# Two attention groups moved in a fused attention, mixture-of-experts and soft-routing kernel

## The chip, the cores and the metric

The kernel runs on one core of a Trainium2 chip, in one launch. The metric is device time in microseconds (us). Before the change the median of three runs is 650.23 us (649.72 to 650.28). The measurement of the changed kernel is set against it.

## What is computed

Three stages follow each other, all in fp32.

```
# attention: 4 batches, 8 heads, 768 positions, 64 per head; chunks of 32 queries
k_ctx = k[chunk start - 16 : chunk end + 8];  k_full = mem_k (8) + k_ctx
a = softmax(q_c @ k_full.T / 8);  out = a @ v_full
# squared-relu layer: x (3072, 512), w_in (512, 2048), w_out (2048, 512)
h = x @ w_in;  g = s * relu(h)**2 + b;  x = g @ w_out
# soft routing: 8 experts with 4 slots each
logits = x @ phi
slot_input = softmax(logits, over tokens).T @ x
slot_out[e] = relu(slot_input[e] @ w1[e]) @ w2[e]
out = softmax(logits, over slots) @ slot_out
```

For the two layers the kernel splits each operand into a high and a low part in the matmul format `float32r`, and a product is three matmuls: high by high, high by low, low by high.

## The kernel before, in words

**Tiling.** The 3072 tokens are six blocks j of 512. Attention is cut into units u: one block and one pair of heads, four units a block, 24 in all. The units of blocks 2 and 3 (8 to 15) are taken in the order of `SEQ`; unit 14 is block 3, head pair 1, unit 16 the first of block 4.

A unit has these parts. Its *scores* (`att_qk`) are 16 small fp32 matmuls, which the profile counts as 32, into one PSUM bank. Then comes the softmax on that bank: `att_top` on VectorE (two small masks where a batch ends, the maximum, the subtraction), the exponent on ScalarE (`att_e`), and `att_norm` on VectorE (sum, epsilon, reciprocal, multiplication). The *turn* (`att_turn`) is four transposes on TensorE, placed by two copies (`att_place`). The *values* (`att_pvmm`) are again 16 matmuls, counted as 32, and one ScalarE copy into x (`att_copy`). `run_bg("qk", u, bank)` issues the scores, the loads of Q and K two units on, and the whole softmax; `run_bg("pv", u, bank)` issues the values, the copy and the load of V two units on; "qktr" is the scores of u with the turn of u - 1 behind them.

**Steps.** Blocks 0 and 1 go through the squared-relu layer in 32 steps n, one for each block and each 128 columns of `w_in`. A step issues on TensorE `mm_h(n)` (12 matmuls of 512 columns into bank 4 or 5), then what attention is due, then `mm_y(n - 1)` (12 matmuls into banks 0 to 3). Between the two lie, for the h of the step, `make_r` (ScalarE), `make_t` (VectorE), `make_high` (ScalarE) and `make_low` (VectorE): the square, biased and split.

**Super blocks.** Blocks 2 and 3 are one 2 by 2 super block (`first_super`), blocks 4 and 5 another (`last_super`). A super block goes through eight pairs p of column blocks by a scheme of seven products of half size in place of eight: a11, s1, s2, s4, s3, a22, a12, six matmuls each (`prod`, with the operands from `x_split`, `x_sum`, `w_sums`, `w_split`). Products add onto each other in PSUM: bank A takes a11, is copied out (c11), takes s2 on top, is copied out (c12), takes s3 on top; bank C takes s1, is copied out (c22), takes s4 on top. The copies c11, c22 and c12 are ScalarE's (L808, L826, L833). The two products of the step before (`pending`) run between.

**Order.** TensorE and SP (the DMA queue's engine) run in written order everywhere. In steps 16 to 27 (`plain_step`) a planner orders the other engines. Steps 28 to 31 (`hand_step`) and the two super blocks stand under a manual schedule of ScalarE, VectorE and GpSimd too: they run in written order. What attention is due in which step is listed in `bg`. The lines around the change are:

```
# hand_step(31), L1343 on
mm_h; w_split(1, 0); make_r; values of unit 16; make_g; mm_y(30)
x_split t2; x_split t3; x_sum t4; w_split(2, 0)
# first_super, p = 0, L807 on
prod a11; c11; x_split t4; w_sums(1); w_split(3, 0); prod s1; c22; w_split(0, 1)
prod s2; c12; w_split(1, 1); scores of 17; prod s4; add; prod s3; add; softmax of 17
mm_y(31); prod a22; prod a12; turn of 17
```

In `hand_step`, values that lead a step's list are issued ahead of `make_g`. In step 28 they would write bank 5; in step 31 they write bank 7.

Of the kernel before, what the change touches and what calls it, by code (L numbers as in the profile page):

```python
# [18 lines left out]
NHP = 4  # L19
# [34 lines left out]
def tile_attention_moe_softmoe(  # L54
# [88 lines left out]
    bank = [ppool.tile([P, 512], F32, name=f"bank{i}", tag=f"bank{i}") for i in range(8)]  # L143
# [69 lines left out]
    def att_qk(u, b):  # L213
        S = b.rearrange("p (t n) -> p t n", t=8)
        qt, kt = qv(u), kv(u)
        for i in range(4):
            for z in range(2):
                for par in range(2):
                    c = 4 * i + 2 * par + z
                    pe.matmul(S[64 * par:64 * par + 64, 2 * i + z, :], lhsT=qt[:, c].rearrange("p h n -> p (h n)"), rhs=kt[:, KG * c:KG * c + 64],  # L220
                              start=True, stop=True)
# [19 lines left out]
    def att_exp(u, b):  # L241
        att_top(u, b)
        att_e(u)
# [11 lines left out]
    def att_norm(u, last=None):  # L255
        att_sum(u)
        att_mul(u, last or dve)
# [137 lines left out]
    def make_g(n):  # L395
        make_t(n)
        make_high(n)
        make_low(n)
# [173 lines left out]
    for u in range(2 * NHP, 4 * NHP + 1):  # L572
        n0 = NF - 4 + 2 * (u - 2 * NHP)
        bg[n0].append(("qk", u))
        bg[n0 + 2].append(("tr", u))
        bg[n0 + (4 if u < 4 * NHP - 2 else 3)].append(("pv", u))
    for step, task in ((3, "log"), (3, "ytr0"), (5, "etr"), (5, "ytr1"), (7, "ytr2"), (7, "ytr3"), (7, "csoft"), (9, "slot")):
        bg[NF + step].append((task, 0))
    for n, tasks in bg.items():
# [5 lines left out]
    def att_next(a):  # L585
        if a + 2 < NB * NHP:
            load_q(a + 2)
            load_k(a + 2)

    def run_bg(task, a, b=None):  # L590
        if task == "qk":
            att_qk(a, b)
            att_next(a)
            att_exp(a, b)
            att_norm(a)
        elif task == "tr":
            att_tr(a, b, a < 2 * NHP)
        elif task == "qktr":
            att_qk(a, b)
            att_next(a)  # L600
            c = mbank()
            att_turn(a - 1, c)
            att_place(a - 1, c)
            att_exp(a, b)
            att_norm(a)
        elif task == "pv":
            att_pv(a, b)
            att_low(a, b)
            if a + 2 < NB * NHP:
                load_v(a + 2)  # L610
        elif task == "log":
            y_logits(a, b)()
        elif task[:3] == "ytr":
            y_tr(int(task[3]), b, "act" if int(task[3]) % 2 else "dve")
        elif task == "etr":
            pe.transpose(b[:, 128:256], lts, ident)
            e_tr(b)
            dve.tensor_copy(lall[:, 4 * a:4 * a + 4, :], b[:, 128:256].rearrange("p (t s) -> p t s", t=4))
        elif task == "csoft":
            c_soft(a)  # L620
        elif task == "slot":
            slots(a, b)
# [138 lines left out]
    def first_super(pending):  # L761
# [41 lines left out]
        for p in range(NPR):  # L803
            c11 = hl(ch[0])[:, p % 2]
            more = p + 1 < NPR
            A, D = yq[0], yq[3]
            prod(A, "a11", "b11", p)  # L807
            act.activation(out=c11, in_=A, func=AF.Copy)  # L808
            if p == 0:
                x_split("t4", 0, 1)  # L810
            if p:
                att_place(4 * NHP + p, D)
                finish(p - 1)
            if p == 1:
                w_split(2, 1)
                evac_spare(yp)
            if p == 5:
                run_bg("csoft", jr)
            if more:
                w_sums(p + 1)  # L820
            w_split(3, p)
            wi_load(p + 2)
            if not more:
                t2_load(0)
            prod(C, "s1", "t1", p)
            act.activation(out=c22, in_=C, func=AF.Copy)  # L826
            w_prep(0, p + 1)
            if not more:
                prep(0)
                x_split("b11", 1, 0)  # L830
                x_split("b11", 1, 1)
            prod(A, "s2", "t2", p, False)
            act.activation(out=c12, in_=A, func=AF.Copy)  # L833
            w_prep(1, p + 1)
            if not more:
                t2_load(1)
            if p:
                run_bg("pv", 4 * NHP + p, B)
            if more:
                att_qk(4 * NHP + p + 1, D)  # L840
                att_next(4 * NHP + p + 1)
                if p:
                    att_exp(4 * NHP + p + 1, D)
                    att_norm(4 * NHP + p + 1)
            pending.pop(0)()
            if p:
                next_load(p, 0)
            prod(C, "s4", "b22", p, False)
            dve.tensor_tensor(out=c12, in0=C, in1=c12, op=ALU.add)
            if not more:  # L850
                x_sum("t1", 1, 0)
                x_sum("t1", 1, 1)
            prod(A, "s3", "t3", p, False)
            dve.tensor_tensor(out=c22, in0=A, in1=c22, op=ALU.add)  # L854
            if p == 0:
                att_exp(4 * NHP + 1, D)
                att_norm(4 * NHP + 1)

            def square2():
                relu(r2, ch[1])  # L860
                times(cur[G2[p]], ch[1], r2)
                if p:
                    w_prep(2, p + 1)

            if p:
                square2()
            if not more:
                t2_load(4)
                prep(1)
                x_split("t1", 1, 0)  # L870
                x_split("t1", 1, 1)
            late = lambda: None
            for t in routing.get(p, ()):
                if t == "log":
                    late = y_logits(jr, D)
                else:
                    run_bg(t, jr, B if t in ("ytr0", "ytr1", "ytr3") else D)
            pending.pop(0)()
            if p:
                next_load(p, 1)  # L880
            else:
                ws_load(R[3], 1)
            if not more:
                t2_load(6)
                t2_load(7)
            prod(A, "a22", "t4", p, False)
            relu(t21, A)
            times(t21, A, t21)
            late()
            prod(B, "a12", "b21", p)  # L890
            if not more:
                t2_load(5)
            dve.tensor_tensor(out=c11, in0=B, in1=c11, op=ALU.add)
            g_high(t21, G[1])
            relu(t11, c11)
            g_low(t21, G[1])
            times(t11, c11, t11)
            if p == 0:
                square2()
            if more:  # L900
                att_turn(4 * NHP + p + 1, D)
            pending.append(lambda p=p: mm_job(yp, cur[R[(2 * p) % 4]], G[1], p == 0, False))
            pending.append(lambda p=p: mm_job(yp, cur[R[(2 * p + 1) % 4]], G[0], False, p == NPR - 1))
# [327 lines left out]
    with tc.manual_schedule(engines={mybir.EngineType.PE, mybir.EngineType.SP}):  # L1231
# [101 lines left out]
        def hand_step(n):  # L1333
            m = n - (NSTEP - 4)
            if m == 0:
                split_wi(n + 1)
                wi_load(0)
                wi_load(1)
                ws_load(R[0], NPR, True)
                ws_load(R[1], 0, True)  # L1340
            split_wo(n)
            sp.dma_start(out=DWS[n % NF], in_=WO[n % 2])
            mm_h(n, (0, 1, 2, 3))  # L1343
            if m == 3:
                w_split(1, 0)
            make_r(n)
            tasks = [lambda t=t, a=a: run_bg(t, a, bank[7] if n == NSTEP - 1 else HB[(n + 1) % 2] if t == "pv" else mbank())
                     for t, a in bg[n]]
            if bg[n][0][0] == "pv":
                tasks.pop(0)()  # L1350
            make_g(n)
            if n + 2 < NSTEP:
                split_wi(n + 2)
            for t in tasks:
                t()
            mm_y(n - 1)
            if m == 0:
                x_sum("t1", 0, 1, pool)
            elif m == 1:
                x_split("t1", 0, 1)  # L1360
            elif m == 2:
                w_sums(0)
                x_sum("t2", 0, 1)
                x_sum("t3", 0, 1)
                x_split("b22", 0, 1)
                w_split(0, 0)
            else:
                x_split("t2", 0, 1)
                x_split("t3", 0, 1)
                x_sum("t4", 0, 1)  # L1370
                w_split(2, 0)
                ws_load(R[2], NPR + 1)
# [258 lines left out]
```

## Time and profile before

| | |
|---|---|
| median of three runs | 650.23 us |
| the profiled execution | 649.8 us, its span 648.0 us |
| TensorE matmul | busy 636.5 us, 98% |
| TensorE weight load | busy 511.6 us, 79%, beside the matmuls |
| VectorE | busy 441.0 us, 68% |
| ScalarE | busy 354.8 us, 55% |
| GpSimd | busy 281.2 us, 43% |
| DMA | 183.33 MB, mean 283 GB/s |
| granted TensorE clock | 0.997 of full speed |
| chain that ended last | TensorE 96%, VectorE 2% |

A matmul's row in the trace is longer than its share of the engine, since matmuls overlap: what one costs is the distance between two starts. In a timeline, rows of one line and one set of tiles that follow without a gap are one row with a count. A bracket at its end gives the engine's idle time before it and what released it. PE is TensorE, PEld its weight loads, DVE is VectorE, ACT ScalarE, POOL GpSimd.

### The profile page before, as it was taken

The page shows a single profiled execution, that of the slowest core. Times are in us where ns is not written, and L with a number is a line of the kernel's source. Part 1 is how long each engine was busy: PE and PEld are TensorE (multiplying, and loading weights), DVE is VectorE, ACT ScalarE, POOL GpSimd, SP SyncE. Part 2 cuts the span into 40 slices and gives each one's busy share as a digit, 9 for nine tenths or more (in the row PEclk, how much of TensorE's full clock was granted, in tenths as well). Part 3 has the DMA queues.
Part 4 walks back from the last instruction along what each step waited for, and adds up shares of the span by engine and source line. Part 5 has one row for each costly group of instructions (what it writes and reads, how often), then busy time and mean ns, then how long its engine had stood idle before and what let it go on. Part 6 is the DMA issues. An engine that isn't in the chain of part 4 may idle for free.

```text
span 648.0 us, 12886 instructions
## 1 busy us (share of the span) xinstructions
PE 636.5 (98%) x4965; PEld 511.6 (79%) x4965; DVE 441.0 (68%) x716; ACT 354.8 (55%) x640; POOL 281.2 (43%) x227
## 2 busy tenths in 40 slices
PE   8999999999999999999999999999999999999995
PEld 7788888888878888888788887888887888886384
DVE  6999989666864678656566587616766889676233
ACT  5898887655554556554354555425654456554232
POOL 5897856343333584643534103454455515320000
PEclk9999999999999999999999999999999999999998
DMA  8998854577746755978754687469999789999998
GB/s 331 408 405 306 307 184 171 170 274 252 262 168 212 286 200 211 332 263 297 285 192 180 218 294 227 183 196 379 333 344 323 243 291 334 331 379 409 406 408 323
DMA packets 59821, 183.33 MB, mean 283 GB/s; under 512 B 6640, under 2 KB 7920, under 8 KB 59760
## 3 DMA queue, kind: packets, MB, share of 16 engines
q1 hardware_dynamic: 59760, 182.51, 77.5%
q8 instruction: 39, 0.64, 0.4%
q14 instruction: 22, 0.18, 0.1%
HBM read 136.35 MB, written 46.14 MB: 282 GB/s over the span
## 4 chain that ended last, share of the span: by engine, by line
PE 96%; DVE 2%; ACT 0%; issue 0%; DVEq 0%; POOL 0%; POOLq 0%
PE bank L407 28%; PE bank L737 24%; PE bank L377 13%; PE bank L995 12%; PE bank L285 3%; PE bank L220 3%; PE bank L1486 2%; PE bank L1445 2%; PE bank L459 2%; PE bank L263 2%; PE bank L433 1%; PE bank L475 1%; PE bank L1515 1%; PE bank L1245 1%; PE bank L513 0%
## 5 line engine op out<-in xcount | busy, mean ns | idle before, releaser
L407 PE MATMUL bank<-g,wo 128*128 128x512 f32 x528 | 130.0, 395 | 0.0
L407 PEld LDWEIGHTS bank<-g,wo 128*128 128x128 f32 x528 | 96.9, 188 | 21.7 <-ACT wi L347 0.8
L377 PE MATMUL bank<-x,wi 128*128 128x512 f32 x384 | 92.8, 390 | 0.0
L377 PEld LDWEIGHTS bank<-x,wi 128*128 128x128 f32 x384 | 71.8, 188 | 15.3 <-DVE x L308 0.4
L385 DVE SCALAR_TENSOR_TENSOR rt<-bank,cons,rt 128x512 f32<-128x512 f32 x32 | 23.8, 745 | 29.1 <-ACT rt L381 28.9
L326 POOL TENSOR_SCALAR sp<-sp 128x512 f32<-128x512 f32 x20 | 43.0, 2174 | 0.0
L366 POOL TENSOR_TENSOR wo<-w,wo 128x512 fp32r<-128x512 f32 x16 | 21.9, 1367 | 45.3 <-ACT wo L362 32.5
L729 POOL TENSOR_TENSOR w14n<-sp6n,w14n 128x512 fp32r<-128x512 f32 x8 | 14.5, 1815 | 46.9 <-ACT w14n L728 46.9
L351 POOL TENSOR_TENSOR wi<-w,wi 128x512 fp32r<-128x512 f32 x17 | 22.4, 1318 | 24.8 <-ACT wi L347 21.3
L347 ACT ACTIVATE wi<-w 128x512 fp32r<-128x512 f32 x32 | 20.1, 629 | 19.9 <-PE bank L377 15.0
L392 DVE SCALAR_TENSOR_TENSOR g<-rt,cons,g 128x512 fp32r<-128x512 f32 x32 | 25.6, 799 | 6.2 <-ACT g L388 5.9
L362 ACT ACTIVATE wo<-w 128x512 fp32r<-128x512 f32 x32 | 20.1, 627 | 16.4 <-PE bank L407 9.0
L285 PEld LDWEIGHTS bank<-pb,v 128*64 128x64 f32 x704 | 22.2, 138 | 8.0 <-issue 2.5
L388 ACT ACTIVATE g<-rt,cons 128x512 fp32r<-128x512 f32 x32 | 23.1, 720 | 9.0 <-DVE rt L385 8.5
L239 ACT ACTIVATE ep<-ep 128x512 f32<-128x512 f32 x22 | 13.9, 632 | 23.1 <-DVE ep L235 23.0
L285 PE MATMUL bank<-pb,v 128*64 128x64 f32 x704 | 25.1, 225 | 0.8 <-ACT pb L273 0.5
L220 PE MATMUL bank<-k,q 128*64 128x64 f32 x704 | 24.8, 226 | 0.0
L752 ACT ACTIVATE rt1n<-y1n 128x1024 f32<-128x1024 f32 x8 | 8.5, 1058 | 29.0 <-DVE y1n L854 29.0
L220 PEld LDWEIGHTS bank<-k,q 128*64 128x64 f32 x704 | 22.9, 141 | 1.4 <-issue 1.3
L381 ACT ACTIVATE rt<-bank 128x512 f32<-128x512 f32 x32 | 18.7, 583 | 6.3 <-PE bank L377 6.1
L985 POOL TENSOR_TENSOR k0n<-sp5n,k0n 128x512 fp32r<-128x512 f32 x6 | 8.2, 1360 | 30.4 <-ACT k0n L984 30.3
L247 DVE TENSOR_REDUCE ast<-ep 128x8 f32<-128x512 f32 x22 | 15.0, 681 | 8.6 <-ACT ep L239 8.2
(696 smaller groups left out, 1742.4 us busy)
## 6 DMA issues: line engine op xcount, KB each, us to landing
v<-vd SPq DMA_DIRECT2D x22, 512.0 KB, 5.1
sp<-wd SPq DMA_DIRECT2D x22, 512.0 KB, 9.3
q<-qd SPq DMA_DIRECT2D x20, 512.0 KB, 7.3
dws<-wo SPq DMA_DIRECT2D x16, 512.0 KB, 6.3
k<-kd SPq DMA_DIRECT2D x22, 332.0 KB, 7.0
wo<-dws SPq DMA_DIRECT2D x12, 512.0 KB, 4.5
dwi<-w SPq DMA_DIRECT2D x16, 256.0 KB, 6.5
dwr<-w SPq DMA_DIRECT2D x16, 256.0 KB, 6.3
```

The lines of the kernel that those rows point to most:

```text
L220: pe.matmul(S[64 * par:64 * par + 64, 2 * i + z, :], lhsT=qt[:, c].rearrange("p h n -> p (h n)"), rhs=kt[:, KG * c:KG * c + 64], start=Tru ...
L285: pe.matmul(b[64 * h:64 * h + 64, 64 * m:64 * m + 64], lhsT=vt[:, m, h, :], rhs=pb[:, m // 2, m % 2, h].rearrange("p z n -> p (z n)"), sta ...
L326: eng.tensor_scalar(out=hv, in0=hv, scalar1=-EXP_TOP, scalar2=EXP_TOP, op0=ALU.max, op1=ALU.min)
L351: (dve if n < NF and n not in (0,) else pool).tensor_tensor(out=r32(t[:, 1]), in0=raw, in1=t[:, 0], op=ALU.subtract)
L366: (dve if n < NF else pool).tensor_tensor(out=r32(t[:, :, 1]), in0=raw, in1=t[:, :, 0], op=ALU.subtract)
L377: pe.matmul(HB[n % 2], lhsT=r32(w[:, a, kt, :]), rhs=r32(x[:, b]), start=(kt == 0 and i == 0), stop=(kt == 3 and i == 2))
L385: dve.scalar_tensor_tensor(out=t, in0=HB[n % 2], scalar=s_col, in1=r, op0=ALU.mult, op1=ALU.mult)
L388: act.activation(out=r32(hl(G[n % 2])[:, 0]), in_=hl(RT[n % 2])[:, 1], func=AF.Identity, bias=b_col)
L392: dve.scalar_tensor_tensor(out=r32(g[:, 1]), in0=t, scalar=b_col, in1=g[:, 0], op0=ALU.add, op1=ALU.subtract)
L407: pe.matmul(yb[dt], lhsT=r32(w[:, dt // 2, a, dt % 2 * 128:dt % 2 * 128 + 128]), rhs=r32(g[:, b]), start=(first and i == 0), stop=(last an ...
L737: pe.matmul(b, lhsT=r32(wv[:, a, kt, :]), rhs=r32(xv[:, c]), start=(first and kt == 0 and i == 0), stop=(kt == 1 and i == 2), skip_group_c ...
L995: pe.matmul(banks[d], lhsT=r32(w[:, a, d * 128:d * 128 + 128]), rhs=r32(g[:, b]), start=(first and i == 0), stop=(last and i == 2), skip_g ...
```

## The change

The values of unit 14 go from step 27 to step 28, whose list then reads values of 14, scores of 16, turn of 15. The scores of unit 17, with the loads and the softmax that `run_bg` issues with them, go from pair 0 of the first super block into step 31: behind the values of unit 16 and ahead of `make_g(31)`. They use bank 6 there in place of bank 7. In the other pairs the four calls are replaced by `run_bg`, which makes the same four in the same order.

```diff
@@ the list of what is due in which step
-        bg[n0 + (4 if u < 4 * NHP - 2 else 3)].append(("pv", u))
+        bg[n0 + (4 if u < 4 * NHP - 1 else 3)].append(("pv", u))
@@ first_super, in pair p, behind prod s2
-            if more:
-                att_qk(4 * NHP + p + 1, D)
-                att_next(4 * NHP + p + 1)
-                if p:
-                    att_exp(4 * NHP + p + 1, D)
-                    att_norm(4 * NHP + p + 1)
+            if more and p:
+                run_bg("qk", 4 * NHP + p + 1, D)
@@ first_super, in pair p, behind prod s3 and its addition
-            if p == 0:
-                att_exp(4 * NHP + 1, D)
-                att_norm(4 * NHP + 1)
-
@@ hand_step(n), m = n - 28
             if bg[n][0][0] == "pv":
                 tasks.pop(0)()
+            if m == 3:
+                run_bg("qk", 4 * NHP + 1, bank[6])
             make_g(n)
```

## Rows read from the trace of the kernel before

**Rows 1.** The page's part 1: engine, busy us (share of the span) and instructions.

```profile
PE 636.5 (98%) x4965; PEld 511.6 (79%) x4965; DVE 441.0 (68%) x716; ACT 354.8 (55%) x640; POOL 281.2 (43%) x227
```

**Rows 2.** Timeline of TensorE, step 31 into pair 1: start us, length us, engine, line, operation, tiles.

```profile
230.10 1.15 PE L285 MATMUL bank<-pb,v 128*64 128x64 f32 x32
231.18 3.02 PE L407 MATMUL bank<-g,wo 128*128 128x512 f32 x12
234.03 0.84 PE L737 MATMUL bank<-w0n,wi0n 128*128 128x512 f32 x3
...
236.75 0.84 PE L737 MATMUL bank<-w4n,wi1n 128*128 128x512 f32 x3
237.43 0.84 PE L737 MATMUL bank<-w11n,wi1n 128*128 128x512 f32 x3
238.20 1.15 PE L220 MATMUL bank<-k,q 128*64 128x64 f32 x32
239.29 0.96 PE L737 MATMUL bank<-w3n,w14n 128*128 128x512 f32 x3
...
252.35 1.15 PE L285 MATMUL bank<-pb,v 128*64 128x64 f32 x32
253.33 1.10 PE L220 MATMUL bank<-k,q 128*64 128x64 f32 x32
254.37 3.02 PE L407 MATMUL bank<-g,yt0n 128*128 128x512 f32 x12
```

**Rows 3.** Timeline of TensorE, steps 27 and 28.

```profile
200.73 2.88 PE L377 MATMUL bank<-x,wi 128*128 128x512 f32 x12
...
207.48 2.88 PE L377 MATMUL bank<-x,wi 128*128 128x512 f32 x12
210.29 1.15 PE L220 MATMUL bank<-k,q 128*64 128x64 f32 x32
```

**Rows 4.** Timeline of GpSimd: the sum t1 in step 28, w14's low before pair 0.

```profile
214.43 1.29 POOL L665 TENSOR_TENSOR x01n<-x01n 128x512 f32<-128x512 f32 x1
...
234.79 1.50 POOL L729 TENSOR_TENSOR w14n<-sp6n,w14n 128x512 fp32r<-128x512 f32 x1 [2.02 <-ACT w14n L728]
```

**Rows 5.** Timeline of VectorE, step 31 into pair 1; idle time and its releaser in brackets.

```profile
231.64 0.75 DVE L385 SCALAR_TENSOR_TENSOR rt<-bank,cons,rt 128x512 f32<-128x512 f32 x1
...
243.10 0.07 DVE L233 MEMSET bank<- 64x8 f32 x1
...
247.23 0.74 DVE L755 SCALAR_TENSOR_TENSOR rt0n<-bank,cons,rt0n 128x512 f32<-128x512 f32 x1
...
254.53 0.07 DVE L233 MEMSET bank<- 64x8 f32 x1 [0.19 <-PE bank L220]
...
259.62 0.68 DVE L849 TENSOR_TENSOR y1n<-bank,y1n 128x512 f32<-128x512 f32 x1
```

**Rows 6.** Timeline of ScalarE, pair 0: c11, t4's high, c22 and c12.

```profile
235.59 0.60 ACT L808 ACTIVATE y0n<-bank 128x512 f32<-128x512 f32 x1 [0.88 <-PE bank L737]
236.87 0.63 ACT L651 ACTIVATE w13n<-x01n 128x512 fp32r<-128x512 f32 x1 [0.68 <-DVE x01n L665]
...
237.93 0.58 ACT L826 ACTIVATE y1n<-bank 128x512 f32<-128x512 f32 x1
...
238.71 0.59 ACT L833 ACTIVATE y1n<-bank 128x512 f32<-128x512 f32 x1
```

**Rows 7.** Timeline of ScalarE, a pair of the other super block: c22.

```profile
509.04 0.58 ACT L1108 ACTIVATE y1n<-bank 128x512 f32<-128x512 f32 x1
```

**Rows 8.** Timeline of TensorE's weight loads (PEld), the same pair: s4.

```profile
509.67 0.53 PEld L737 LDWEIGHTS bank<-w3n,w14n 128*128 128x128 f32 x3 [0.40 <-ACT y1n L1108]
```

**Rows 9.** Stretches at the end: length, busy us (instructions) by engine, clock, DMA share, GB/s.

```profile
640.00:644.00 4.00, 1.66 (x6) 1.05 (x6) 2.34 (x5) 1.61 (x4) 0.00 (x0) 1.00 0.73 289
...
645.00:648.00 3.00, 0.00 (x0) 0.00 (x0) 0.00 (x0) 0.00 (x0) 0.00 (x0) 0.50 0.51 202
```

**Rows 10.** Timeline of TensorE at the end.

```profile
641.57 0.63 PE L1515 MATMUL bank<-w4nn,s 128*128 128x512 f32 x2
```

## The prediction

> **What bounds the kernel now.** The page comes first, for the share of each engine. TensorE is busy for 636.5 of 648.0 us [rows 1], and no other engine comes near. So a change of the order pays or costs only as far as it closes or opens gaps in TensorE's queue, and the other engines count where TensorE waits for them. Next I read TensorE's timeline around the changed steps, for what a small group of matmuls costs beside its neighbours. It has no gap there: each start follows the one before by a fixed step. Three 512-column matmuls take 0.68 us, 236.75 to 237.43 [rows 2], that is 0.227 each, and twelve 2.72. The reader is to see that a group of 32 small attention matmuls costs more than its own time: it makes its neighbours start late. Last I read VectorE's and ScalarE's timelines of the same stretch, for how long before TensorE needs it each product is ready. There the trouble lies.
>
> **Part 1: values of unit 14 from step 27 to step 28.** Step 27 takes 200.73 to 207.48, 6.75 us [rows 3], against 2 x 2.72 = 5.44 without the group; leaving, it saves 1.31. In step 28 it comes to stand before the scores, at 210.29 [rows 3]. How such neighbours run shows in pair 1 of the super block: values 252.35 to 253.33, 0.98, then scores to 254.37, 1.03 [rows 2] (differences are of unrounded starts). A lone scores group takes 1.08 (238.20 to 239.29, [rows 2]), and so does that of step 28 now. So step 28 grows by 0.98 + 1.03 - 1.08 = 0.93, and the part gives 0.37 us. Its followers: one ScalarE copy of some 0.6 us goes in ahead of step 28's biased squares, which are used a step later, so that whole step covers it. GpSimd's sum t1 (214.43 to 215.72, [rows 4]) needs the copied values. The values start at 210.29, where the scores do now; with 0.98 of matmuls, their pipeline's end and 0.6 of copy they are there by about 212.1, over 2 us ahead of the sum. The load of V for unit 16 goes behind it on SP's queue and is wanted in step 31, three steps on. If such cover failed, it would cost at most the 0.6 of the copy. No queue gains a wait that TensorE sees: 0.37 saved, bounds 0 and 0.37.
>
> **Part 2: first scores of the super block from pair 0 to step 31, on TensorE.** In pair 0 they stand alone: 1.08, plus 0.09 on entry (237.43 to 238.20 is 0.77 in place of 0.68) and 0.13 on leaving (three matmuls at 239.29 last 0.96 in place of 0.84; 2.85 in place of 2.72 for twelve from 231.18 to 234.03 has the same tail) [rows 2]: 1.30 go. Beside the values they cost what pair 1 shows: 0.98 and 1.03, 2.01 together, against 1.08 for values alone (230.10 to 231.18): 0.93 come. Another 0.37 saved.
>
> **Part 2 on the other engines.** The whole task moves, not its matmuls alone: the loads of Q and K for unit 19 too (on SP they pass the stores of the splits and the load of `wo` that stand between; the first of these, the store of w14, waits for w14's low on GpSimd, 236.29 [rows 4], longer than these loads wait for the scores' matmuls, so they hold it back by nothing), and all of its softmax. It is written ahead of step 31's squares, and VectorE, ScalarE and GpSimd run in written order here. In pair 0 this softmax lay behind the last addition, and TensorE went on with products that needed none of it. Now `make_t(31)` is queued behind it on VectorE; `make_high(31)` waits for that on ScalarE; and behind it stand the splits of t2 and t3, of sp6, the copies c11, c22 and c12. Two of these copies empty a PSUM bank that TensorE is about to add into: s2 goes on top of c11's bank, s4 on top of c22's.
>
> I keep the profile's time axis, on which part 1 shifts all alike. The values start at 230.10, the scores at 231.08, y(30) at 232.11, a11 at 234.97, s1 at 236.33, s2 at 237.69, s4 at 239.05: these are TensorE's times if nothing stalls.
> - In pair 1 the first memset starts 1.20 us after the first score matmul (254.53 after 253.33) [rows 2, 5]: here at 231.08 + 1.20 = 232.28.
> - The softmax holds VectorE 247.23 - 243.10 = 4.13 us [rows 5], ScalarE's exponent within it. So `make_t(31)` starts at 236.41 and not at 231.64 [rows 5]: 4.77 later.
> - c11 starts at 235.59 now, after ScalarE waited 0.88 for TensorE [rows 6]. Without that it could have come at 234.71. Then 234.71 + 4.77 = 239.48, and it ends at 240.08: s2 starts 0.05 later, at 240.13, and has waited 2.4 us.
> - t4's high starts right after t4's sum on VectorE, its releaser, at 236.87, and c22 follows behind w15's high at 237.93 [rows 6]. That chain hangs on `make_t` without slack, so c22 moves by the full 4.77, to 242.70, and with its 0.58 ends at 243.28.
> - s4 can start 0.05 later, at 243.33, and not at 239.05: 4.28 lost, s2's wait included. That TensorE does wait for this kind of copy is seen in the other super block: the weight load of s4 idles 0.40 us until the copy of 509.04 to 509.62 is done, and starts at 509.67 [rows 7, 8]. After the idle time the first matmuls come late as after a small group: 0.12 more.
> - Next in line is c12, 238.71 + 4.77 = 243.48, done at 244.07 [rows 6]; s3 wants its bank at 243.33 + 0.12 + 1.36 = 244.81 and doesn't wait. w14's low, which s4 reads too, is done on GpSimd at 236.29 now [rows 4] and would be at 241.06: covered. y(31) comes after s3, and its squares have long been ready. What leaves VectorE at 243.10 held up nothing on TensorE: no gain there.
>
> The unsure term is the length of the softmax: 4.13 in pair 0, 259.62 - 254.53 = 5.09 in pair 1 [rows 5], where other work ran beside it. In step 31 ScalarE and GpSimd have little, as in pair 0; I take 4.13 and keep 5.09, 0.96 more, for the upper end. The lower end is a softmax whose part behind c11 is absorbed, the wait of s2 alone: 2.4.
>
> **The sum.** -0.37 - 0.37 + 4.28 + 0.12 = +3.66. TensorE has no later gap in which this could vanish. The profiled execution took 649.8 us (648.0 of span and 1.8 around it), so 653.5; the median of the runs shown, 650.23, lies 0.43 above it and gives 653.9. I say 653.7.
>
> **The rivals.**
> - *Nothing stalls, the joining alone counts* (not slower). It would be so if the squares of step 31 reached VectorE ahead of the softmax, or it were finished in time. Place: `make_t(31)`. Point of decision: c22 ends at 238.51 now and s4 wants its bank at 239.05 after the change [rows 2, 6], so a delay of up to 0.5 us is free; I count 4.77. Time: 649.8 - 0.74 = 649.1, with the median 649.5. For it: a full TensorE gains by each joined group. Against it: the order that the rows of VectorE show in pair 0 is the written one, and ScalarE sat behind VectorE there as well.
> - *Only s2's wait shows.* If t4's sum and high got ahead of c22's copy, or were short, s4 would not wait again: -0.74 + 2.4 + 0.12 = +1.8, 651.6 to 652.0. Against it: ScalarE already idles 0.68 for t4's sum [rows 6], so this link has no slack.
> - *The clock falls in the gaps.* TensorE would be idle for 2.4 us and again for 1.7 (s2 from 240.13 lasts 1.36 + 0.12, to 241.61; s4 starts at 243.33). At the very end the last matmuls start at 641.57 and are over by 642.2, and the granted clock is 1.00 up to 644 and 0.50 from 645 [rows 9, 10]: idleness ended in the lower level, 1.2 GHz, though after a longer stretch than either gap. Should it fall at s4, each us of matmuls costs one more: at least the 1.36 of s4, at most the some 8 us to the end of pair 0, so 655 to 662; nearest to the row is that it doesn't fall. The Trainium skill, in TensorE: Matmul & The Clock Gate, Part 1: The HAM clock gate, says that the throttled state is the default and that activity releases it, which speaks for this rival. By that rule the last rows agree, and no run here shows a gap of this size inside dense work.
> - *A longer softmax*, by 0.96: 654.7.
>
> **How the numbers follow.** The forecast, 653.2 to 654.8 with the longer softmax, gets 0.78; s2's wait alone 0.06; nothing stalls 0.11; the clock 0.05. The range 651.6 to 655.6 holds the first two and the mildest clock. Up to 0.2%, 1.3 us, a measurement of this kernel can't tell from no change. The case without a stall gives 0.7 and so counts mostly as no change: faster 0.03, same 0.09, slower 0.88.
>
> **What would show it.** Step 27 takes 5.44 us and step 28 0.93 more than now. In step 31 values and scores stand together in 2.01. On VectorE the softmax stands ahead of `make_t(31)`, which starts some 5.1 us after the scores do. On TensorE there are two gaps in pair 0, about 2.4 us before s2 and 1.7 before s4, each ended by ScalarE's copy (c11, then c22). After that all is as before and late by about 3.7. I am wrong if `make_t(31)` precedes the softmax, if the gaps lie elsewhere, or if granted clock falls in them.

## The result: slower by 0.62%, and the profile after

The changed kernel takes 653.83 us (median of 6 runs; before 649.98, 6 runs). The ratio is 1.0062, with a 95% interval of 1.0051 to 1.0073: 3.3 to 4.7 us, clear of no change. The profiled execution took 653.8 us with a span of 652.0, 4.0 more than the 648.0 before. In the table of experiments below, one of the eleven executions of the version with the softmax back in pair 0 took 3602 us, against 648.3 to 650.1 for the other ten, and its ratio leaves that one out.

First the page's parts that answer to rows 1: the span, and each engine's busy time.

```profile
span 652.0 us, 12883 instructions
...
PE 636.6 (98%) x4965; PEld 511.5 (78%) x4965; DVE 441.7 (68%) x716; ACT 354.6 (54%) x640; POOL 280.9 (43%) x227
```

TensorE has as much to do as before, to 0.1 us, and no other engine has more than 0.7 us more. So the 4 us are idle time of TensorE, or what lies ahead of its first work. The waits of TensorE between 225 and 262 us (line waited for, us in total, times, longest) name it at once; the kernel before has no wait in that stretch.

```profile
PE bank L737 <- ACT y0n L808: 2.1, 1, 2.1
PE bank L737 <- ACT y1n L826: 1.6, 1, 1.6
```

These are the two copies of the prediction, c11 (L808) and c22 (L826), with 2.1 and 1.6 us. The timeline of TensorE shows where: step 27 starts at 201.24 here, step 28 at 206.68, step 31's values at 230.23, and pair 1's at 256.43.

```profile
201.24 2.88 PE L377 MATMUL bank<-x,wi 128*128 128x512 f32 x12
...
206.68 2.88 PE L377 MATMUL bank<-x,wi 128*128 128x512 f32 x12
209.49 1.15 PE L285 MATMUL bank<-pb,v 128*64 128x64 f32 x32
210.48 1.10 PE L220 MATMUL bank<-k,q 128*64 128x64 f32 x32
...
214.74 2.88 PE L377 MATMUL bank<-x,wi 128*128 128x512 f32 x12
...
230.23 1.15 PE L285 MATMUL bank<-pb,v 128*64 128x64 f32 x32
231.22 1.10 PE L220 MATMUL bank<-k,q 128*64 128x64 f32 x32
232.25 3.02 PE L407 MATMUL bank<-g,wo 128*128 128x512 f32 x12
...
240.13 0.97 PE L737 MATMUL bank<-w4n,wi1n 128*128 128x512 f32 x3 [2.15 <-ACT y0n L808]
...
243.44 0.96 PE L737 MATMUL bank<-w3n,w14n 128*128 128x512 f32 x3 [1.65 <-ACT y1n L826]
...
256.43 1.15 PE L285 MATMUL bank<-pb,v 128*64 128x64 f32 x32
```

Both joined groups are there. Step 27 lasts 5.44 us and step 28 8.06, against 6.75 [rows 3] and 7.13; in the kernel before, step 28 ends where step 29 starts:

```profile
214.61 2.88 PE L377 MATMUL bank<-x,wi 128*128 128x512 f32 x12
```

Values and scores stand side by side in step 31, 230.23 to 232.25, 2.01 together. Then TensorE idles 2.15 before s2, for c11, and 1.65 before s4, for c22. VectorE (DVE) shows why: the softmax of unit 17 starts at 232.41 (the first mask) and lasts to the start of the square of step 31, L385, at 236.54; in the kernel before that square stood at 231.64 [rows 5].

```profile
232.41 0.07 DVE L233 MEMSET bank<- 64x8 f32 x1 [0.83 <-PE bank L220]
...
236.54 0.74 DVE L385 SCALAR_TENSOR_TENSOR rt<-bank,cons,rt 128x512 f32<-128x512 f32 x1
...
239.95 1.77 DVE L665 TENSOR_TENSOR x01n<-x03n,x01n 128x512 f32<-128x512 f32 x1
```

On ScalarE the bias of that square (L388) starts after 2.59 us of idleness, c11 (L808) follows at 239.51, t4's high (L651, `w13n`) after another 1.68 for the sum on VectorE, and c22 (L826) at 242.81. In rows 6 these stand at 235.59, 236.87 and 237.93.

```profile
237.32 0.72 ACT L388 ACTIVATE g<-rt,cons 128x512 fp32r<-128x512 f32 x1 [2.59 <-DVE rt L385]
...
239.51 0.57 ACT L808 ACTIVATE y0n<-bank 128x512 f32<-128x512 f32 x1
241.75 0.63 ACT L651 ACTIVATE w13n<-x01n 128x512 fp32r<-128x512 f32 x1 [1.68 <-DVE x01n L665]
...
242.81 0.58 ACT L826 ACTIVATE y1n<-bank 128x512 f32<-128x512 f32 x1
...
243.60 0.59 ACT L833 ACTIVATE y1n<-bank 128x512 f32<-128x512 f32 x1
```

From the start of step 27 to the values in pair 1 it is 256.43 - 201.24 = 55.19 us, before 252.35 - 200.73 = 51.62 [rows 2, 3]: 3.57 more, where the prediction's sum says 3.66. This stretch holds both parts and leaves out the start and end of the execution, which vary: the profiled execution's remaining 0.4 us lie there (step 27 itself starts 0.51 later). The experiments are compared by it too.

The granted clock stayed at 1.00 in the stretches with the gaps (length, busy us and instructions of PE, PEld, DVE, ACT and POOL, clock, DMA share, GB/s):

```profile
236.00:241.00 5.00, 2.85 (x13) 2.05 (x12) 4.21 (x6) 2.76 (x5) 1.32 (x1) 1.00 0.62 231
242.00:248.00 6.00, 4.56 (x20) 3.78 (x21) 2.57 (x3) 2.70 (x6) 5.84 (x7) 1.00 0.67 240
```

### The profile page after: what moved, and what is told of

Same layout as the page of the kernel before. It is cut to its first block, busy times and chain, and to the rows that moved or that the text cites. A ratio compares the mean times of both kernels' runs of the same rounds, so it can differ in the third digit from the quotient of the medians.

```text
span 652.0 us, 12883 instructions
## 1 busy us (share of the span) xinstructions
PE 636.6 (98%) x4965; PEld 511.5 (78%) x4965; DVE 441.7 (68%) x716; ACT 354.6 (54%) x640; POOL 280.9 (43%) x227
## 4 chain that ended last, share of the span: by engine, by line
PE 60%; DVE 1%; ACT 1%; issue 0%; DVEq 0%; ACTq 0%
PE bank L737 22%; PE bank L407 14%; PE bank L987 12%; PE bank L1480 2%; PE bank L1439 2%; PE bank L459 1%; PE bank L285 1%; PE bank L1509 1%; PE bank L220 1%; PE bank L475 1%; PE bank L433 1%; PE bank L513 0%; PE bank L263 0%; PE bank L1458 0%; DVE x11n L755 0%
## 5 line engine op out<-in xcount | busy, mean ns | idle before, releaser
L385 DVE SCALAR_TENSOR_TENSOR rt<-bank,cons,rt 128x512 f32<-128x512 f32 x32 | 23.9, 746 | 28.5 <-ACT rt L381 28.4
L388 ACT ACTIVATE g<-rt,cons 128x512 fp32r<-128x512 f32 x32 | 23.1, 721 | 10.2 <-DVE rt L385 9.8
```

Source lines behind the costliest of these rows:

```text
L385: dve.scalar_tensor_tensor(out=t, in0=HB[n % 2], scalar=s_col, in1=r, op0=ALU.mult, op1=ALU.mult)
L388: act.activation(out=r32(hl(G[n % 2])[:, 0]), in_=hl(RT[n % 2])[:, 1], func=AF.Identity, bias=b_col)
```

## The experiments

Theory: the loss is the softmax of unit 17 ahead of step 31's squares and splits, by way of the copies c11, c22; the two joined groups give 0.37 us each. The rivals are the matmuls or loads that moved, an effect of the two parts on each other, and the clock. The stretch is that from step 27 to pair 1's values.

| kernel | run against before | 95% interval | stretch, us | against 51.62 |
|---|---|---|---|---|
| changed | 1.0062 | 1.0051 to 1.0073 | 55.19 | +3.57 |
| part 1 alone | 0.9997 | 0.9988 to 1.0006 | 51.22 | -0.40 |
| part 2 alone | 1.0067 | 1.0049 to 1.0084 | 55.55 | +3.93 |
| softmax back in pair 0 | 0.9989 | 0.9980 to 0.9998 | 50.87 | -0.75 |
| squares first | 1.0085 | 1.0071 to 1.0099 | 58.11 | +6.49 |
| t4's split behind c22 | 1.0034 | 1.0021 to 1.0047 | 53.62 | +2.00 |
| no softmax of unit 17 | 0.9991 | 0.9981 to 1.0001 | 50.78 | -0.84 |
| squares first, t4 behind c12 | 1.0010 | 1.0000 to 1.0019 | 52.15 | +0.53 |
| squares first, gap filled (28) | 1.0099 | 1.0082 to 1.0116 | 58.39 | +6.77 |
| squares first, gap filled (14) | 1.0057 | 1.0040 to 1.0073 | 55.60 | +3.98 |

**Part 1 alone.** The kernel before with

```diff
-        bg[n0 + (4 if u < 4 * NHP - 2 else 3)].append(("pv", u))
+        bg[n0 + (4 if u < 4 * NHP - 1 else 3)].append(("pv", u))
```

> Part 1 alone: the kernel before with the values of unit 14 in step 28. Theory (each joined group gives 0.37 us, and nothing waits for what moved): 0.37 us less than before, step 27 at 5.44 us, step 28 0.93 longer, no gap of TensorE between steps 26 and pair 1. Rival (the copy, the sum t1 on GpSimd or the load of V are late behind the moved values): up to 0.6 us more than the 0.37 less, with a gap in steps 28 to 30.

TensorE's timeline, the starts of steps 27 and 28, the values of unit 14 and the start of step 29:

```profile
200.20 2.88 PE L377 MATMUL bank<-x,wi 128*128 128x512 f32 x12
...
205.64 2.88 PE L377 MATMUL bank<-x,wi 128*128 128x512 f32 x12
208.46 1.15 PE L285 MATMUL bank<-pb,v 128*64 128x64 f32 x32
...
213.70 2.88 PE L377 MATMUL bank<-x,wi 128*128 128x512 f32 x12
```

Step 27 takes 5.44 us, step 28 8.06; the stretch is 0.40 shorter, and TensorE waits nowhere in it. The run's ratio alone, with 0.09% to either side, can't tell a gain of 0.06% from none: here the trace decides.

**Part 2 alone.** The changed kernel with the line above undone.

> Part 2 alone: the changed kernel with the values of unit 14 left in step 27. Theory (the softmax ahead of step 31's squares makes the copies c11 and c22 late): the whole loss is here, +4.0 us over before (4.28 + 0.12 - 0.37), with the same two gaps in pair 0 as in the changed kernel, 2.1 and 1.6 us, ended by ScalarE's copies. Rival (the two parts disturb each other, since both leave more for VectorE and ScalarE in steps 28 to 31): clearly less than 4.0, the gaps smaller.

TensorE's waits, 225 to 262 us:

```profile
PE bank L737 <- ACT y0n L808: 2.1, 1, 2.1
PE bank L737 <- ACT y1n L826: 1.6, 1, 1.6
```

The same two gaps to within 0.02 us, and +3.93 in the stretch: the parts add up, 3.93 - 0.40 = 3.53 against 3.57. So part 1 has no share in the loss, and the rival of a mutual effect is out.

**Softmax back in pair 0.** The changed kernel with

```diff
             if m == 3:
-                run_bg("qk", 4 * NHP + 1, bank[6])
+                att_qk(4 * NHP + 1, bank[7])
+                att_next(4 * NHP + 1)
             make_g(n)
...
             dve.tensor_tensor(out=c22, in0=A, in1=c22, op=ALU.add)
+            if p == 0:
+                att_exp(4 * NHP + 1, D)
+                att_norm(4 * NHP + 1)
```

and with bank 6 for the values of unit 16.

> The changed kernel with the scores' matmuls and the loads of unit 17 in step 31, but the softmax back in pair 0 behind the addition that follows s3; the values of unit 16 take bank 6 and these scores bank 7, so that bank 6 is free for s1. Theory (it is the softmax's place alone): no gap in pair 0, c11 and c22 on time, both joined groups' gain left: 0.74 us less than before, 4.4 less than the changed kernel. Rival (the scores' matmuls or the early loads in step 31 are what costs): still 2 us or more over before.

TensorE: the scores in step 31, s2 at 237.52, s4 at 238.88:

```profile
230.92 1.10 PE L220 MATMUL bank<-k,q 128*64 128x64 f32 x32
...
237.52 0.84 PE L737 MATMUL bank<-w4n,wi1n 128*128 128x512 f32 x3
...
238.88 0.84 PE L737 MATMUL bank<-w3n,w14n 128*128 128x512 f32 x3
```

Both gaps are gone, with matmuls, loads and joined groups where the change put them: -0.75 in the stretch, as expected to 0.01, and a ratio of 0.9989, below 1 with its whole interval. This is the version that beats both kernels. The place of the softmax is the cause, not that of the scores.

**No softmax of unit 17.**

```diff
-                run_bg("qk", 4 * NHP + 1, bank[6])
+                att_qk(4 * NHP + 1, bank[6])
+                att_next(4 * NHP + 1)
```

> The changed kernel without the softmax of unit 17 (its masks, maximum, subtraction, exponent, sum and multiplication are left out; scores, loads, turn and values stay). Theory (the softmax in front of the squares is the whole loss; scores in bank 6 and the early loads cost nothing): no gap in pair 0, 0.74 us less than before, the same as with the softmax back in pair 0. Rival (early loads or bank 6 cost something): above that by what they cost.

-0.84 in the stretch, no wait of TensorE in it. Bank 6 and the early loads cost nothing, and with the run before it is seen that the softmax costs TensorE next to nothing in pair 0 (0.09).

**Squares first.**

```diff
+            make_g(n)
             if m == 3:
                 run_bg("qk", 4 * NHP + 1, bank[6])
-            make_g(n)
```

> The changed kernel with make_g(31) written ahead of the scores and softmax of unit 17; TensorE's order is unchanged. Theory in its narrow form (the late make_t(31) alone does it): the gaps go, 0.74 less than before. Theory in its wide form (anything of 4.1 us on VectorE ahead of the splits of t2 and t3 and the sum t4 makes c22 late, since c22 stands behind t4's high on ScalarE): make_t(31) is on time at about 5 us earlier than in the changed kernel, the gap before s2 shrinks to about 0.5 us, but the one before s4 grows to about 2.9, and the loss is 3.1 us over before, only 0.6 less than in the changed kernel.

A miss in size: 655.49 us, +5.5 us by the ratio, where the wide form said +3.1. The profiled execution is the longest of the four (654.45 to 656.14), so its stretch shows more, +6.49. VectorE does what was meant: the square (L385) at 231.04, the softmax from 233.41, t2's low (`w11n`) only at 237.54.

```profile
231.04 0.75 DVE L385 SCALAR_TENSOR_TENSOR rt<-bank,cons,rt 128x512 f32<-128x512 f32 x1
...
233.41 0.07 DVE L233 MEMSET bank<- 64x8 f32 x1
...
237.54 1.77 DVE L655 TENSOR_TENSOR w11n<-x01n,w11n 128x512 fp32r<-128x512 f32 x1
```

The waits of TensorE, 225 to 262 us:

```profile
PE bank L737 <- ACT y1n L826: 3.2, 1, 3.2
PE bank L737 <- ACT y0n L808: 0.4, 1, 0.4
PE bank L737 <- DVE w11n L655: 0.3, 1, 0.3
```

So the narrow form falls: the square is in time, and the loss grows. The wide form has its gaps, 0.4 before s2 and 3.2 before s4 (expected 0.5 and 2.9). Two things it did not have. One is a wait of 0.33 inside s2 for t2's low, which took 1.77 us in place of 0.68. GpSimd was at work on w14's low from 237.37 on, and VectorE's subtraction began behind that, at 237.54:

```profile
237.37 1.39 POOL L729 TENSOR_TENSOR w14n<-sp6n,w14n 128x512 fp32r<-128x512 f32 x1 [5.22 <-ACT w14n L728]
```

In the kernel before, t2's low (`w11n`) ran while GpSimd was idle, and t3's low (`w12n`), begun ahead of GpSimd's w14's low (234.79 [rows 4]), was as short beside it:

```profile
233.85 0.68 DVE L655 TENSOR_TENSOR w11n<-x01n,w11n 128x512 fp32r<-128x512 f32 x1
234.45 0.68 DVE L655 TENSOR_TENSOR w12n<-x01n,w12n 128x512 fp32r<-128x512 f32 x1
```

The other is the clock. TensorE's timeline, s4's and s3's twelve matmuls from 243.30 to 248.59, and three stretches (columns as above):

```profile
243.30 1.65 PE L737 MATMUL bank<-w3n,w14n 128*128 128x512 f32 x3 [3.21 <-ACT y1n L826]
...
247.31 1.45 PE L737 MATMUL bank<-w12n,w14n 128*128 128x512 f32 x3
248.59 2.93 PE L407 MATMUL bank<-g,wo 128*128 128x512 f32 x12
```

```profile
236.00:241.00 5.00, 3.36 (x13) 1.81 (x11) 4.90 (x7) 1.77 (x4) 3.55 (x3) 1.00 0.78 295
242.00:248.00 6.00, 4.70 (x11) 3.73 (x12) 1.75 (x2) 2.56 (x6) 4.48 (x5) 0.50 0.57 182
249.00:255.00 6.00, 6.00 (x30) 4.92 (x30) 1.91 (x3) 1.26 (x2) 0.00 (x0) 1.00 0.56 209
```

After the gap a matmul takes 0.427 us (1.28 for the three from 247.31) and not 0.227, at a granted clock of 0.50, the 1.2 GHz level; s4 and s3 take 5.29 us in place of some 2.85. At 249 the clock is back at 1.00. The rival that the prediction priced for the changed kernel came true in this execution, whose last gap is longer.

**t4's split behind c22**, the softmax still ahead of the squares:

```diff
-            if p == 0:
-                x_split("t4", 0, 1)
...
             act.activation(out=c22, in_=C, func=AF.Copy)
+            if p == 0:
+                x_split("t4", 0, 1)
             w_prep(0, p + 1)
```

> The changed kernel with t4's split in pair 0 written behind the copy c22 in place of ahead of it; the softmax stays ahead of the squares. Theory (two separate waits, one for c11 behind the squares, one for c22 behind t4's high): the gap before s2 stays at 2.1 us, the one before s4 goes, and since c12 now stands behind t4's high a small one of about 0.3 may appear before s3: 1.8 to 2.2 us over before. Rival (c22 is late for the squares alone, t4's high doesn't matter): no change from the changed kernel, +3.7.

TensorE at s2 (its first half, from 239.40) and s4 (240.89):

```profile
239.40 0.97 PE L737 MATMUL bank<-w4n,wi1n 128*128 128x512 f32 x3 [2.15 <-ACT y0n L808]
...
240.89 0.86 PE L737 MATMUL bank<-w3n,w14n 128*128 128x512 f32 x3
```

The gap before s2 stays at 2.15, s4 follows without one, s3 starts 0.2 late behind c12, and the stretch is +2.00, all as expected. Two copies, two waits: c22 was late by standing behind t4's high, which waits for VectorE's sum.

**Squares first, t4's split behind c12.** Both orders changed:

```diff
+            make_g(n)
             if m == 3:
                 run_bg("qk", 4 * NHP + 1, bank[6])
-            make_g(n)
...
-            if p == 0:
-                x_split("t4", 0, 1)
...
             act.activation(out=c12, in_=A, func=AF.Copy)
+            if p == 0:
+                x_split("t4", 0, 1)
             w_prep(1, p + 1)
```

> The kernel with the squares first, and t4's split in pair 0 moved behind the copy c12, so that c11, c22 and c12 stand behind nothing that waits for the sum t4. Theory (a copy that empties a bank TensorE adds into is late only for what stands ahead of it on ScalarE): c22 and c12 are on time, the 3.2 us gap before s4 goes and with it the lower clock; what is left is s2, which in the kernel with the squares first lost 1.3 us (c11 0.4 us late, then t2's low on VectorE 0.3 late, each with a slow restart). So 1.3 - 0.74 = 0.6 us over before. Rival (any softmax in step 31 costs TensorE several us wherever the copies stand): over 3 us.

TensorE, s2 in three pieces and s4 at 239.54:

```profile
237.42 0.98 PE L737 MATMUL bank<-w4n,wi1n 128*128 128x512 f32 x3 [0.41 <-ACT y0n L808]
238.24 0.40 PE L737 MATMUL bank<-w11n,wi1n 128*128 128x512 f32 x1
238.96 0.74 PE L737 MATMUL bank<-w11n,wi1n 128*128 128x512 f32 x2 [0.33 <-DVE w11n L655]
239.54 0.86 PE L737 MATMUL bank<-w3n,w14n 128*128 128x512 f32 x3
```

Only s2's two small waits are left; +0.53 and a ratio of 1.0010, as expected. The whole softmax sits in step 31 here, and nearly all of the loss is gone.

**The gap filled.** Squares first, and between s2 and s4 on TensorE

```diff
+            if p == 0:
+                for _ in range(28):
+                    pe.matmul(B[:, 0:128], lhsT=ident, rhs=ident, start=True, stop=True)
             prod(C, "s4", "b22", p, False)
```

> The kernel with the squares first, with 28 small matmuls (128 columns, on constants, into a bank that is free there, 0.11 us each, 3.1 together) put on TensorE between s2 and s4, where it sat idle for 3.2 us and the granted clock then was 0.50 for 6.8 us. The result isn't changed by them. Theory (half clock on s4 and s3 is 2.4 us of that kernel's loss; the fill takes idle time alone): granted clock stays 1.00, s4 starts at the same time behind the same copy, s4 and s3 take 2.8 us and not 5.3, and the run is 2.4 us shorter than the one without the fill: 3.1 to 3.4 over before. Rival (the slow matmuls have another cause, or the fill delays s4): no shorter than without it.

A miss by its own fault: each of these fp32 matmuls is two records and took 0.22 us, so the fill lasted 6.2 us, not 3.1, and delayed s4 itself. The clock did stay at 1.00, and s4 and s3 took 2.82. With 14:

> As the run before, with 14 small matmuls in place of 28: there each took 0.22 us and not 0.11 (two records each), so that the fill lasted 6.2 us and held s4 up by 2.9. Fourteen last 3.1 and end before the copy c22 is done. Theory (the half clock is 2.4 us of the loss with the squares first): granted clock 1.00 throughout, s4 starts 0.05 us after c22, s4 and s3 together 2.8 us and not 5.3; 2.4 less than with the idle gap, some 653.2 or 3.3 us over before. Rival (the fill only moves the cost): 655 or more.

The fill (L846), s4 from 242.76, s3's end at 245.61, and the stretch that had 0.50:

```profile
239.39 3.29 PE L846 MATMUL bank<-cons 128*128 128x128 f32 x28
242.76 0.96 PE L737 MATMUL bank<-w3n,w14n 128*128 128x512 f32 x3
...
245.61 2.88 PE L407 MATMUL bank<-g,wo 128*128 128x512 f32 x12
```

```profile
242.00:248.00 6.00, 5.92 (x30) 4.84 (x29) 2.24 (x3) 2.02 (x5) 3.95 (x4) 1.00 0.56 171
```

s4 and s3 take 2.85 us, and the stretch is 58.11 - 55.60 = 2.51 shorter than with TensorE idle, for the same late copy; the run came out at 653.72 where 653.2 was expected. So some 2.5 us of the +6.49 in the profiled execution with the squares first was the lower clock, and the rest, +3.98, the late copies and t2's late low. Over all executions the fill gave less: the medians, 655.49 and 653.72, lie 1.8 apart.

## Why the prediction was right

The time (653.7 for 653.83) and the way hold, and so do the steps. That the two times agree to 0.13 us is luck in part: the interval of the loss, 3.3 to 4.7 us, is some ten times as wide, and 0.4 us of the profiled execution's 4.0 lie outside the steps that the prediction added up. What bears it out is the stretch, 3.57 for 3.66. In order:

- *The joined groups, 0.37 each.* Part 1 alone gives 0.40 in the stretch; with the softmax back in pair 0 both give 0.75. Right.
- *The copy, sum t1 and the load of V are covered.* No wait of TensorE with part 1 alone. Right.
- *The softmax holds VectorE 4.13 us.* 232.41 to 236.54 is 4.13. The upper end, 5.09, was not needed: ScalarE and GpSimd were idle beside it, as in pair 0.
- *`make_t(31)` 4.77 later.* On an axis that starts with step 31's values (230.10 [rows 2], 230.23) it is 236.54 - 231.64 - 0.13 = 4.77: 4.13 for the softmax, and 0.64 more because VectorE, in written order, stands ahead of it until the scores are there. The text's last part says 5.1 us after the scores; its own working gives 5.33, and 5.32 is measured. That was a slip.
- *s2 at 240.13 and s4 at 243.33.* On the same axis 240.00 and 243.31, 2.31 and 4.26 later than without a stall (2.44 and 4.28 in the prediction). The trace's gaps, 2.15 and 1.65, are smaller because a row ends later than the next can start; each is ended by the copy named. Right.
- *c12 and w14's low are covered.* c12 ends at 244.19, and the twelve matmuls of s4 and s3 run from 243.44 without a wait (y(31) at 246.31). Right.
- *Next to no gain in pair 0 from the softmax that left.* Without the softmax at all it is 0.09 in the stretch, small against the terms of the sum.
- *The rivals.* That nothing stalls is what the softmax back in pair 0 does, 0.75 faster: the rival was the right time for another order. "Only s2's wait" is what t4's split behind c22 does: the prediction had +1.8, the stretch says +2.00, with 0.2 before s3 that the prediction had not. The clock did not fall in the profiled execution of the change. But of the ten executions of the change and of part 2 alone, two (655.40 and 656.09 us) have a mean granted clock of 0.992 and 0.994, the other eight, at 0.997 to 0.998, take 653.0 to 654.0. That would fit a lower clock after the gaps in those two. Neither was the profiled one, so this stays open; if it did fall there, the prediction's chance of 0.05 for this rival was low.

The Trainium skill, in TensorE: Matmul & The Clock Gate, Part 1: The HAM clock gate, has the throttled state as the default, released by activity. The squares-first kernel agrees with that rule: 0.50 after its longest gap, and 1.00 with the gap filled.

What the prediction did not see was that the change was one edit from a gain: the joined matmuls pay, and only the softmax had to stay where it was.

## What to carry to other kernels

When a task is moved to win time on the busiest engine, move only the instructions of that engine, and leave the task's other work where its queues have room. On engines that run in written order, ask what stands behind the moved work and follow it to the copies that free a PSUM bank: the busiest engine waits for those, though they cost it nothing themselves. A copy that the busiest engine waits for belongs ahead of anything that can itself wait on a third engine; with the squares first, that alone took the stretch from +6.49 (2.5 of it the lower clock) to +0.53 us.

## What was not expected of the hardware

- In the profiled execution with the squares first, three waits of 0.41, 0.33 and 3.21 us, with s2 between them, brought TensorE to the lower clock, and s4 and s3 lost 2.4 us more; 2.15 and 1.65 did not in the profiled execution of the change.
- Idle time filled with matmuls whose result nobody reads gave 2.5 us back in the profiled execution, at no cost to the work behind them, as long as the fill ended before the copy did.
- VectorE's subtraction of 512 columns takes 0.68 us alone and took 1.77 where it began behind GpSimd's subtraction of the same size (237.54 and 237.37 above). Where it began ahead of GpSimd's (234.45 and 234.79) it took 0.68. So an order that lets GpSimd's start first cost a microsecond here.
- An fp32 matmul of 128 columns by 128 takes 0.22 us (28 of them 6.2), about twice what a transpose of that width takes in the same kernel (four in 0.35 to 0.44 us).
